# A Sin activation with its quarter turn as a number, and a skip term seeded into the bank by TensorE

## The chip, the cores and the metric

The kernel runs on one core of a Trainium2 chip. The metric is the device time of one launch in microseconds. The kernel before takes 934.82 us (median of three runs, 934.5 to 937.22).

## The reference

One block of a network on 2048 positions of 640 channels, all in fp32: an adaptive layer norm, a state-space convolution with a skip term, then a second adaptive norm and a gated feed-forward part.

```python
mod = (_silu(c) @ w_mod).reshape(c.shape[0], 6, 1, -1)          # sa, ca, ga, sb, cb, gb
h = _layernorm(x) * (1 + ca) + sa
x = x + ga * conv(h)
h = _layernorm(x) * (1 + cb) + sb
x = x + gb * ((_silu(h @ w1) * (h @ w3)) @ w2)

def conv(u):                                                     # u: [1, L, D]
    dt = exp(log_dt)[:, None]
    P = exp((dt * A)[:, :, None] * arange(L))                    # A, B, C complex, [D, 128]
    K = einsum("dn,dnl,dn->dl", C, P, dt * B).real               # one filter of length L per channel
    return causal_convolution(u, K) + u * Dskip                  # by FFT in the reference
```

Adding `Dskip` of a channel to the first tap of its filter, `K[d, 0]`, gives the same as the term `u * Dskip`.

## The kernel before

The engines are TensorE (PE; its weight loads are PEld), VectorE (DVE), ScalarE (ACT), GpSimd (POOL) and SyncE (SP, which issues most transfers). The program has two halves. Up to about 365 us it makes the filters and convolves; behind that it runs the feed-forward part in fp32r matmuls. The change touches the first half alone.

The filters are made in 40 steps (`NS`) of 16 channels (`SD`), and each step is cut into parts with two-letter names:

- `PH`: POOL multiplies the angles as integers (tile `ph`, 16 x 64 per partition). `AB`: ACT takes the absolute value into `cs`. `CO`: ACT turns `cs` into cosines in place, as Sin of a quarter turn minus the angle (`cosine`, L581). `SI`: ACT makes the sines in `ph`.
- `PA`, `XA`, `PQ`, `XQ`: PE multiplies out the exponents (banks `pa`, `pq`, which share the bank tagged B), and ACT takes Exp of them into the table `A`.
- `E1`, `E2`, `A1`, `A2`: DVE multiplies table and angles, into `E` (real parts) and `A` (imaginary parts).
- `kg` (`kgen`, L607): PE sums over the 128 states, in 32 fp32 matmuls with 32 weight columns and 64 moving columns, into one bank `pk` of [128, 4, 64]. Partition `dq * 32 + a`, group `g`, column `b` holds tap `64 a + b` (in the order of the tables) of channel `4 g + dq`.
- `K` (`k1evac`, L618): DVE adds the skip term to column 0 of each group, then multiplies the bank by the gate into the tile `K1`. `dz` is zero except on partitions 0, 32, 64 and 96, where it holds D.
- `pt`, `uk`: PE and ACT transform and store the filter; the `st`, `kc`, `T`, `Y`, `iv`, `zt` parts (tiles `p`, `kc`, `T`, `Y`, `pz`, `zt`) convolve the chunk of channels that was made before.

`pk` has one bank, so `kg` of a step waits until `K` of the step before has read it. Some parts have dummy matmuls ahead of them (`warm`: identity times identity, 128x128, into the bank that is about to be filled), to keep PE busy.

The order is written out by hand. `FRONT` is a list of words for the start (to about 128 us), which mixes the first steps with the setup, and `ROUND` is a list for a steady round of four steps. A word is a part's name, the step in the round and, behind a slash, the number of dummies. In `ROUND` the four sums stand as `kg+5`, `kg+6/1`, `kg+7` and `kg+8/2`: two with dummies and two without. `keep`, `act` and `acopy` fix each instruction at its place in its engine's order.

```python
def warm(t, n):
    ...
    for _ in range(n):
        Po.matmul(out[:, :P] if len(out.shape) == 2 else out, ident, ident, start=True, stop=True)
```

Of the kernel before, what the change touches and what calls it, by code (L numbers as in the profile page):

```python
# [9 lines left out]
F32 = mybir.dt.float32  # L10
F32R = mybir.dt.float32r
I32 = mybir.dt.int32
AF = mybir.ActivationFunctionType
OP = mybir.AluOpType
# [3 lines left out]
P = 128  # L18
# [15 lines left out]
TURN = 4294967296.0  # L34
# [51 lines left out]
def bc(ap, axis, n):  # L86
    v = ap.unsqueeze(axis)
    shape = list(v.shape)
    shape[axis] = n
    return v.broadcast_to(shape)  # L90
# [18 lines left out]
def tile_kernel(ctx: ExitStack, tc: tile.TileContext, a):  # L109
    nc = tc.nc  # L110
    V, S, G, PE = nc.vector, nc.scalar, nc.gpsimd, nc.tensor
# [7 lines left out]
    ident = cp.tile([P, P], F32, name="ident")  # L119
# [11 lines left out]
    def keep(ins):  # L131

        return tc.keep_in_program_order(ins) if in_order[0] else ins

    def act(*args, **kw):

        return tc.keep_in_program_order(S.activation(*args, **kw))  # L137
# [20 lines left out]
    kp = ssm.enter_context(tc.tile_pool(name="kp", bufs=1, side="right"))  # L158
# [2 lines left out]
    gaT = kp.tile([P, D // 4], F32, name="gaT")  # L161
    dz = kp.tile([P, D // 4], F32, name="dz")
    V.memset(dz, 0.0)
    hp = kp.tile([P, 1], F32, name="hp")
    V.memset(hp, math.pi / 2)
    sc = kp.tile([P, KD], F32, name="sc")
    cT = kp.tile([P, KD], F32, name="cT")
    uk = kp.tile([P, 3, NA, DC], F32, name="uk")
# [16 lines left out]
    pm_ = pre.enter_context(tc.tile_pool(name="pm_", bufs=1, side="right"))  # L185
# [7 lines left out]
    selx, stepx = selstep[:, :NA], selstep[:, NA:]  # L193
    s1r, c1, c1c, one4 = misc[:, :2 * NA], misc[:, 2 * NA:4 * NA], misc[:, P:P + 1], misc[:, P + 1:P + 2]
    toq, tog = misc[:, P + 2:2 * P + 2], misc[:, 2 * P + 2:]
    tiny = pm_.tile([P, 1], F32, name="tiny")
    V.memset(tiny, -1e-35)


    flat = [uk[:, i].rearrange("p f d -> p (f d)") for i in range(3)]  # L200
# [46 lines left out]
    def warm(t, n):  # L247

        out = t if len(t.shape) == 2 else t[:, 0] if t.shape[2] >= P else t[:, :P // t.shape[2]]
        for _ in range(n):  # L250
            Po.matmul(out[:, :P] if len(out.shape) == 2 else out, ident, ident, start=True, stop=True)

    class Polar:
# [46 lines left out]
        def turn(self):  # L300
            act(self.m, self.m, AF.Arctan)
            act(self.ag, self.g_r, AF.Sign, scale=-1.0)
            act(self.ai, self.g_i, AF.Sign, scale=-1.0, bias=tiny)

        def round1(self):
            Vo.scalar_tensor_tensor(self.aim, self.aim, 0.25 / math.pi, self.dtc, op0=OP.mult, op1=OP.mult)
# [220 lines left out]
    ph, cs, AA, EC, PK, K1 = {}, {}, {}, {}, {}, {}  # L527
# [51 lines left out]
        cs[s] = c  # L579

    def cosine(s):  # L581
        act(cs[s], cs[s], AF.Sin, scale=-2 * math.pi / TURN, bias=hp)

    def sine(s):
        sn = ph[s].bitcast(F32)
# [21 lines left out]
    def kgen(s, n=0):  # L607
        E, A = EC.pop(s), AA.pop(s)
        pk = psS.tile([P, SD // 4, NB], F32, name="pk", tag="pk", bufs=1)
        warm(pk, n)  # L610
        for g in range(SD // 4):
            for st, x in enumerate((E, A)):
                for dq in range(4):
                    keep(PE.matmul(pk[dq * 32:dq * 32 + 32, g, :], x[:, g * 4 + dq, 1, :], x[:, g * 4 + dq, 0:3:2, :],  # L614
                                   start=(st == 0), stop=(st == 1), tile_position=(0, dq * 32)))
        PK[s] = pk

    def k1evac(s):  # L618
        dst = tp.tile([P, SD // 4, NB], F32, name="K1", bufs=3)
        pk = PK.pop(s)  # L620
        keep(V.tensor_tensor(pk[:, :, 0], pk[:, :, 0], dz[:, s * 4:s * 4 + 4], op=OP.add))
        keep(V.tensor_tensor(dst, pk, bc(gaT[:, s * 4:s * 4 + 4], 2, NB), op=OP.mult))
        K1[s] = dst

# [193 lines left out]
    def conv_part(fn):  # L818
        return lambda k, *n: fn((k - LAG) // 8, (k - LAG) % 8, *n)

    parts = {"PH": phases, "AB": absph, "CO": cosine, "SI": sine, "PA": lambda k, n=0: exp_fast((k,), "B", n), "XA": fast,
             "PQ": lambda k, n=0: exp_slow((k,), "B", n), "XQ": slow, "E1": real1, "E2": real2, "A1": imag1, "A2": imag2,
             "kg": kgen, "K": k1evac, "pt": k_stage1, "uk": k_out}
    conv = {"st": conv_part(stage2), "kc": conv_part(k_copy), "T": conv_part(products), "Y": conv_part(sums),
            "iv": conv_part(inverse1), "zt": conv_part(z_store)}
# [93 lines left out]
    for word in FRONT:  # L919
# [3 lines left out]
        name, k = main.split("+") if "+" in main else (main, None)  # L923
# [48 lines left out]
    for rnd in range(NS // EB + 3):  # L972
        for word in ROUND:
            word, _, idle = word.partition("/")
            name, k = word[:2].rstrip("+-"), EB * rnd + int(word[len(word[:2].rstrip("+-")):])
# [60 lines left out]
    V, S, G, PE = (InOrder(tc, e, (in_order,)) for e in (V, S, G, PE))  # L1036
# [503 lines left out]
    for pair in range(2):  # L1540
# [24 lines left out]
        for n, f in enumerate(simple):  # L1565
            hA[f] = h_tile()
            ws = ws or plain_weights(f, ends if pair == 0 and n == 1 else None)
            end = plain("A", f, hA[f], ws, pair == 0, *((lambda: turn(4, 0, 2), lambda: turn(3, 1)) if n == 3 else ()))
            if n < len(simple) - 1:
                ws = None  # L1570
            todo = side.pop(0) if side else None
            if todo:
                with tc.issue_after(end.ins):
                    todo()
            if pair == 0 and n == 1:
                with tc.issue_after(power[0].ins):
                    for j, (x, z, st) in enumerate(early):
                        G.dma_start(xs[j], x)
# [103 lines left out]
```

## Time and profile before

| | us |
|---|---|
| median of the runs | 934.82 |
| span of the profiled execution (the page states no time beside it) | 932.9 |
| stretch from 201.3 to 227.9, one round of four steps | 26.6 |
| busy in that round: ACT, PE, DVE, POOL | 26.18, 25.28, 24.64, 14.87 |
| cosine, 40 ACTIVATEs on [128, 1024] | 45.3 busy, 1.153 each |
| addition of `dz` into `pk`, 40 on DVE | 6.4 busy, 0.159 each |
| the 2560 matmul rows of `pk` (two rows for each fp32 matmul) | 78.8 busy |

A row of the timeline gives the start, the duration, the engine, the line, the operation and the tiles, with the idle time before it and what ended that in brackets. Matmuls overlap in the pipeline, so what one costs is read from the start of one row to the start of the next, not from its duration. A row of the chain gives a start, a length and what the end of the program hung on there.

### The profile page before, as it was taken

The page shows a single profiled execution, that of the slowest core. Times are in us where ns is not written, and L with a number is a line of the kernel's source. Part 1 is how long each engine was busy: PE and PEld are TensorE (multiplying, and loading weights), DVE is VectorE, ACT ScalarE, POOL GpSimd, SP SyncE. Part 2 cuts the span into 40 slices and gives each one's busy share as a digit, 9 for nine tenths or more (in the row PEclk, how much of TensorE's full clock was granted, in tenths as well). Part 3 has the DMA queues.
Part 4 walks back from the last instruction along what each step waited for, and adds up shares of the span by engine and source line. Part 5 has one row for each costly group of instructions (what it writes and reads, how often), then busy time and mean ns, then how long its engine had stood idle before and what let it go on. Part 6 is the DMA issues. An engine that isn't in the chain of part 4 may idle for free.

```text
span 932.9 us, 21160 instructions
## 1 busy us (share of the span) xinstructions
PE 894.6 (96%) x8482; PEld 699.1 (75%) x8482; DVE 692.8 (74%) x1251; ACT 552.7 (59%) x810; POOL 282.3 (30%) x282
## 2 busy tenths in 40 slices
PE   5999889999999999999999999999999999999998
PEld 3776667767777766678888887778888888888886
DVE  6699889999999967676666656686876766664665
ACT  4899899999999843464433323466643333333432
POOL 3633465555556312134222200111632222200000
PEclk9999999999999999999999999999999999999999
DMA  8755888665655987853113117984322211203453
GB/s 253 243 198 201 264 230 223 171 162 153 177 155 149 230 223 245 211 212 99 56 49 97 55 45 201 271 258 158 86 70 85 84 57 57 57 29 99 141 169 114
DMA packets 103703, 140.79 MB, mean 151 GB/s; under 512 B 20612, under 2 KB 62788, under 8 KB 103604
## 3 DMA queue, kind: packets, MB, share of 16 engines
q1 hardware_dynamic: 99772, 129.32, 47.8%
q0 software_dynamic: 2368, 7.77, 2.6%
q10 hardware_dynamic: 1464, 2.34, 0.8%
q8 instruction: 67, 1.10, 0.5%
q14 instruction: 32, 0.26, 0.1%
HBM read 107.94 MB, written 31.46 MB: 149 GB/s over the span
## 4 chain that ended last, share of the span: by engine, by line
PE 72%; ACT 14%; DVE 5%; DMA 4%; issue 3%; SPq 1%; DVEq 0%; ACTq 0%
PE ps L103 56%; PE p L672 4%; ACT cs L137 3%; PE pz L721 3%; ACT A L137 3%; ACT ph L137 2%; PE pm L103 2%; ACT L137 2%; PE pk L614 1%; PE pq L552 1%; PE pa L541 1%; ACT kc L140 1%; DVE uk L103 1%; SPq L103 1%; ACT uk L140 1%
## 5 line engine op out<-in xcount | busy, mean ns | idle before, releaser
L103 DVE TENSOR_TENSOR s<-ps,s 128x512 f32<-128x512 f32 x138 | 94.9, 687 | 80.2 <-PE ps L103 79.7
L566 POOL TENSOR_TENSOR ph<-thi,iota 128x1024 int32<-128x1024 int32 x40 | 98.0, 2451 | 129.5 <-DVE A L604 77.5
L103 DVE TENSOR_TENSOR gl<-rw,gh 128x640 fp32r<-128x640 f32 x87 | 78.0, 897 | 64.2 <-ACT gh L103 64.2
L103 ACT CAST gh<-rw 128x640 fp32r<-128x640 f32 x87 | 63.3, 727 | 101.8 <-PE ps L103 61.5
L103 POOL TENSOR_TENSOR S<-rw 128x256 f32<-128x256 f32 x46 | 36.6, 798 | 170.7 <-DVE S0l L103 151.5
L103 PE MATMUL ps<-xA,gh 128*128 128x512 f32 x280 | 87.9, 392 | 0.1
L103 PE MATMUL ps<-gh,uh 128*128 128x512 f32 x224 | 87.5, 391 | 0.0
L103 PE MATMUL ps<-gl,uh 128*128 128x512 f32 x224 | 87.2, 389 | 0.0
L103 PE MATMUL ps<-gh,ul 128*128 128x512 f32 x208 | 81.1, 390 | 0.0
L672 PE MATMUL p<-uk,s 128*64 128x256 f32 x640 | 77.1, 383 | 0.9 <-issue 0.9
L103 PEld LDWEIGHTS ps<-xA,gh 128*128 128x128 f32 x280 | 52.1, 188 | 12.8 <-ACT xA L103 0.8
L672 PEld LDWEIGHTS p<-uk,s 128*64 128x64 f32 x640 | 43.4, 137 | 22.5 <-issue 3.4
L103 PE MATMUL ps<-xA,gl 128*128 128x512 f32 x140 | 54.5, 390 | 0.0
L103 ACT ACTIVATE s<-ps 128x512 f32<-128x512 f32 (+1 forms) x33 | 19.7, 598 | 50.5 <-PE ps L103 50.5
L600 DVE TENSOR_TENSOR A<-A,ph 128x1024 f32<-128x1024 f32 x40 | 49.0, 1226 | 0.0
L721 PE MATMUL pz<-Y,i 64*128 64x128 f32 x640 | 45.5, 281 | 3.6 <-ACT zt L140 2.0
L721 PEld LDWEIGHTS pz<-Y,i 64*128 64x128 f32 x640 | 39.3, 187 | 12.8 <-issue 7.3
L593 DVE TENSOR_TENSOR E<-A,cs 128x1024 f32<-128x1024 f32 x40 | 48.6, 1216 | 0.4
L103 PEld LDWEIGHTS ps<-gl,uh 128*128 128x128 f32 x224 | 42.1, 188 | 9.0
L103 PEld LDWEIGHTS ps<-gh,uh 128*128 128x128 f32 x224 | 42.1, 188 | 8.7
L137 ACT ACTIVATE cs<-cs,hp 128x1024 f32<-128x1024 f32 x40 | 45.3, 1153 | 0.2
L570 POOL TENSOR_TENSOR ph<-ph,phi 128x512 int32<-128x512 int32 x40 | 44.5, 1115 | 2.6
(244 smaller groups left out, 2301.6 us busy)
## 6 DMA issues: line engine op xcount, KB each, us to landing
rw<-in_w_dram SPq DMA_DIRECT2D x52, 320.0 KB, 3.0
us<-u SPq DMA_DIRECT2D x16, 640.0 KB, 4.5
s<-in_s_dram SPq DMA_DIRECT2D x40, 256.0 KB, 3.4
i<-in_i_dram SPq DMA_DIRECT2D x40, 256.0 KB, 4.0
rw<-in_wg_dram SPq DMA_DIRECT2D x31, 320.0 KB, 3.0
rw<-in_wu_dram SPq DMA_DIRECT2D x28, 320.0 KB, 3.5
uk<-us SPq DMA_DIRECT2D x32, 256.0 KB, 8.1
zs<-zt SPq DMA_DIRECT2D x32, 256.0 KB, 4.1
```

Of the source, the lines that this page charges most:

```text
L103: ins = fn(*args, **kw)
L137: return tc.keep_in_program_order(S.activation(*args, **kw))
L140: return tc.keep_in_program_order(S.copy(out, in_))
L541: keep(PE.matmul(pA[s][:, rr, :], la[r, t, :], r2[r, js, :].rearrange("p j b -> p (j b)"), start=True, stop=True, tile_position=(r.start, 0)))
L552: keep(PE.matmul(pQ[s][:, rr, :256], w[r, t, :], bc(sel[r, js], 2, NA) if i else r1[r, js, :], start=(i == 0), stop=(i == 1), tile_positio ...
L566: keep(G.tensor_tensor(p, bc(thi[:, s * SD:s * SD + SD], 2, NPH), bc(iota, 1, SD), op=OP.mult))
L570: keep(G.tensor_tensor(p[:, :, :NA], p[:, :, :NA], bc(phi[:, s * SD:s * SD + SD], 2, NA), op=OP.add))
L593: keep(V.tensor_tensor(EC[s][:, :, 1:3, :], AA[s][:, :, 1:3, :], mid(cs[s]), op=OP.mult))
L600: keep(V.tensor_tensor(A[:, :, 1:3, :], A[:, :, 1:3, :], mid(ph[s]), op=OP.mult))
L614: keep(PE.matmul(pk[dq * 32:dq * 32 + 32, g, :], x[:, g * 4 + dq, 1, :], x[:, g * 4 + dq, 0:3:2, :], start=(st == 0), stop=(st == 1), tile ...
L672: keep(PE.matmul(p2[par * 64:par * 64 + 64, pi, c, :], s2[:, pi * 2 + par, c * 64:c * 64 + 64], uk[:, 0:kn + 1:kn, f, :], start=True, stop ...
L721: ins = keep(PE.matmul(pz[:, par, (g % 2) * 2 + pi, :], i1[r, pi, c, :], Y[r, pi, c, :], start=(c == 0), stop=(c == 1), tile_position=(par ...
```

## The change

Three edits. The cosine's quarter turn becomes a number in the instruction, and so does the tiny bias of a Sign; the tiles `hp` and `tiny` that held them, and their memsets, go. DVE's addition of `dz` goes. In its place a matmul of the identity (weights) and four columns of `dz` writes the skip term into column 0 of each group of `pk`, with the flag that starts a sum over the whole bank; the 32 matmuls behind it add to the bank and none of them starts a sum.

```diff
-    hp = kp.tile([P, 1], F32, name="hp")
-    V.memset(hp, math.pi / 2)
...
-    tiny = pm_.tile([P, 1], F32, name="tiny")
-    V.memset(tiny, -1e-35)
...
-            act(self.ai, self.g_i, AF.Sign, scale=-1.0, bias=tiny)
+            act(self.ai, self.g_i, AF.Sign, scale=-1.0, bias=-1e-35)
...
-        act(cs[s], cs[s], AF.Sin, scale=-2 * math.pi / TURN, bias=hp)
+        act(cs[s], cs[s], AF.Sin, scale=-2 * math.pi / TURN, bias=math.pi / 2)
...
         warm(pk, n)
+        keep(PE.matmul(pk[:, :, 0], ident, dz[:, s * 4:s * 4 + 4], start=True, stop=True))
         for g in range(SD // 4):
             for st, x in enumerate((E, A)):
                 for dq in range(4):
                     keep(PE.matmul(pk[dq * 32:dq * 32 + 32, g, :], x[:, g * 4 + dq, 1, :], x[:, g * 4 + dq, 0:3:2, :],
-                                   start=(st == 0), stop=(st == 1), tile_position=(0, dq * 32)))
+                                   start=False, stop=(st == 1), tile_position=(0, dq * 32),
+                                   skip_group_check=True))
...
         pk = PK.pop(s)
-        keep(V.tensor_tensor(pk[:, :, 0], pk[:, :, 0], dz[:, s * 4:s * 4 + 4], op=OP.add))
         keep(V.tensor_tensor(dst, pk, bc(gaT[:, s * 4:s * 4 + 4], 2, NB), op=OP.mult))
```

No other instruction changes its place. On PE, at a sum without dummies in a steady round, there stood, behind ACT's release of the bank for `pa`:

```order
L541 MATMUL pa<-r_96,la 128x512 [waits Activation_49]
L541 MATMUL pa<-r_96,la 128x512
L614 MATMUL pk<-E 32x64 [waits DVE_49]
L614 MATMUL pk<-E 32x64 x3
L614 MATMUL pk<-A 32x64 x4
```

and now stands:

```order
L537 MATMUL pa<-r_94,la 128x512 [waits Activation_49]
L537 MATMUL pa<-r_94,la 128x512
L607 MATMUL pk<-dz,ident 128x4 [waits DVE_49]
L611 MATMUL pk<-E 32x64 x4
L611 MATMUL pk<-A 32x64 x4
```

The wait for DVE has gone over to the new matmul, and the sum follows it without a wait of its own. On DVE, at the evacuation of one step, there stood:

```order
L593 TENSOR_TENSOR E<-A,cs 128x16x64 [waits PE_49,Activation_49]
L621 TENSOR_TENSOR pk<-pk,dz 128x4 [waits PE_49]
L622 TENSOR_TENSOR K_3510<-pk,gaT 128x256 [waits DVE_49]
L689 TENSOR_TENSOR T<-p_3463,kc 128x512 [waits PE_49,Activation_49]
L690 TENSOR_TENSOR p_3463<-p_3463,kc 128x4x128 [waits DVE_49]
```

and now, at the same step:

```order
L589 TENSOR_TENSOR E<-A,cs 128x16x64 [waits PE_49,Activation_49]
L619 TENSOR_TENSOR K_3507<-pk,gaT 128x256 [waits PE_49]
L686 TENSOR_TENSOR T<-p_3460,kc 128x512 [waits PE_49,Activation_49]
L687 TENSOR_TENSOR p_3460<-p_3460,kc 128x4x128 [waits DVE_49]
L693 TENSOR_TENSOR Y<-T,p_3460 128x2x128 [waits DVE_49]
```

The multiplication by the gate now waits for PE itself.

## The prediction

> **What bounds the kernel now.** I read the page first, then the busy times by stretch, then the chain of work that ended last, and after that the timeline of one round, engine by engine.
>
> ```profile
> span 932.9 us, 21160 instructions
> ```
>
> All that is edited lies in the first 335 us. So the sum is made by stretches there, and what comes later is taken to move as one piece. The page gives a span of 932.9 us and no time of its own for the profiled execution; the median of the runs is 934.82 us, 1.9 us longer, and I add the sum to that median.
>
> ```profile
> 64.00:100.00 36.00, 34.09 (x622) 24.97 (x626) 35.52 (x72) 35.77 (x47) 13.42 (x13) 1.00 0.50 185
> 201.30:227.90 26.60, 25.28 (x489) 19.11 (x490) 24.64 (x40) 26.18 (x32) 14.87 (x9) 1.00 0.58 157
> 307.80:335.00 27.20, 25.71 (x502) 19.95 (x502) 23.38 (x41) 16.98 (x21) 4.19 (x7) 1.00 0.91 224
> ```
>
> The columns are the stretch, its length, and then the busy time of PE, PEld, DVE, ACT and POOL. From 64 to 100 us DVE and ACT are both full. In a steady round (four steps in 26.6 us) ACT is busy 26.18 and PE 25.28: two engines compete to be the bound, and the chain must say how.
>
> ```profile
> 59.20 2.10 ACT cs L137 x2
> ...
> 118.32 3.14 ACT cs L137 x3
> ...
> 131.59 1.03 PE pk L614 x64
> ...
> 139.74 0.42 PE pk L103 x2
> 140.16 1.03 PE pk L614 x64
> ...
> 159.84 0.59 issue
> ...
> 167.14 1.03 PE pk L614 x64
> ...
> 174.69 1.28 ACT L137
> ...
> 217.35 1.16 PE pz L721 x16
> ...
> 219.97 0.42 PE pk L103 x2
> 220.39 1.03 PE pk L614 x64
> ...
> 224.91 0.44 PE pq L552 x4
> 225.38 0.60 ACT A L137
> ...
> 307.81 1.28 ACT L137
> ```
>
> From 129.6 to 172 us the chain lies almost wholly on PE and holds six of the blocks named `pk`, from the one at 131.59 to the one at 167.14. From the table load at 174.69 to the one at 307.81 there are five equal rounds of 133.12 / 5 = 26.62 us. In each the chain is on ACT for the sines and cosines, then on PE from `pz` (217.35) to the end of `pq` (224.91 + 0.44) with one `pk` block, then on ACT again.
>
> **The change part by part.**
>
> *The cosine.* Forty ACTIVATEs lose the column `hp` as an operand.
>
> ```profile
> L137 ACT ACTIVATE cs<-cs,hp 128x1024 f32<-128x1024 f32 x40 | 45.3, 1153 | 0.2
> L137 ACT ACTIVATE cs<-ph 128x1024 f32<-128x1024 int32 x40 | 42.1, 1053 | 1.1 <-POOL ph L570 0.8 <-DVE E L596 0.3
> 208.88 1.15 ACT L137 ACTIVATE cs<-cs,hp 128x1024 f32<-128x1024 f32 x1
> 209.93 1.06 ACT L137 ACTIVATE cs<-ph 128x1024 f32<-128x1024 int32 x1
> 210.87 0.58 ACT L140 COPY kc<-p 128x512 f32<-128x512 f32 x1
> ```
>
> The absolute value, of the same size and without a column, takes 1053 ns against 1153. From start to start it is 1.05 us after the cosine (208.88 to 209.93) and 0.94 after the absolute value, so a cosine gives back about 0.10 us (the trace has no cosine with a number for its bias; at worst it gives nothing) of ACT's time, 0.38 in a round of four, all of it in the stretch where the chain is on ACT. The two Sign instructions with `tiny` gain as little each, and the two MEMSETs stand at the start, where DVE has its first loads to wait for: I cost both at nothing, and 0.2 us if that is wrong.
>
> *DVE's addition of D.* Forty small additions go.
>
> ```profile
> 87.52 0.16 DVE L621 TENSOR_TENSOR pk<-pk,dz 128x4 f32<-128x4 f32 x1
> 87.71 0.42 DVE L622 TENSOR_TENSOR K<-pk,gaT 128x256 f32<-128x256 f32 x1
> 82.00:106.50 24.50, 0.47 (x3) 1.00 0.55 188
> ```
>
> Each holds DVE for 0.19 us (87.52 to 87.71). In the steady rounds DVE has 2 us to spare, so 0.76 us a round buys nothing there. Where DVE is full it counts: three of them stand between 82 and 106.5 us.
>
> *TensorE's seed.* One matmul is added ahead of each `pk` block: 128x128 identity as weights, four columns of `dz`. The profile has no such row; the nearest are the matmuls with one column and the dummies (each fp32 matmul shows as two rows).
>
> ```profile
> 27.12 0.61 PE L103 MATMUL pm<-misc,part 128*128 128x1 f32 x4
> 27.58 0.47 PE L103 MATMUL pa<-ident 128*128 128x128 f32 x2
> ...
> 114.20 0.83 PE L103 MATMUL pm<-misc,part 128*128 128x1 f32 x6
> 114.95 0.39 PE L552 MATMUL pq<-r,la 64*128 64x256 f32 x2
> ...
> 206.41 0.71 PE L103 MATMUL pk<-ident 128*128 128x128 f32 x4
> 207.06 0.32 PE L614 MATMUL pk<-E 128*32 128x64 f32 x8
> ```
>
> Two one-column matmuls take 0.46 us when a matmul of the same tile follows (27.12 to 27.58), 0.23 each. Three take 0.75 when another tile shape follows (114.20 to 114.95), so the last costs 0.75 - 0.46 = 0.29. A block without dummies ahead of it pays that: I take 0.30. One dummy of 128 columns takes 0.42 with the change of shape behind it (219.97 to 220.39), two take 0.65 (206.41 to 207.06). So a further wide matmul costs 0.23, and ending on a narrow one saves 0.42 - 0.29 = 0.13: behind a dummy the seed costs about 0.11. The bounds are 0.11 to 0.42 for a lone seed and 0.02 to 0.23 behind a dummy, and I take the values of the narrow rows because four columns are nearest to one. A round has two of each kind: 2 x 0.30 + 2 x 0.11 = 0.82 us. The wait for DVE's reading of the bank of the step before moves from the block to the seed, one matmul earlier, so nothing new is waited for, and DVE now frees the bank 0.19 us sooner: no cost.
>
> The Trainium skill's page "TensorEngine Tiling (Array Packing)", under Key Properties, says that a change of tiling mode drains TensorE. By that rule a lone seed pays one drain more than before, which is what speaks against this change; it gives no price, the step from 0.23 to 0.29 and 0.42 above is how this trace shows it, and the sum stays as it is.
>
> *What PE has to spare.* In a round:
>
> ```profile
> 216.45 0.50 PE L541 MATMUL pa<-r,la 64*128 64x512 f32 x2 [0.23 <-ACT A L137]
> 217.35 1.16 PE L721 MATMUL pz<-Y,i 64*128 64x128 f32 x16 [0.40 <-ACT zt L140]
> 218.28 0.39 PE L552 MATMUL pq<-r,la 64*128 64x256 f32 x2
> 219.47 0.50 PE L541 MATMUL pa<-r,la 64*128 64x512 f32 x2 [0.69 <-ACT A L137]
> 217.19 1.04 ACT L137 ACTIVATE A<-pa 128x1024 f32<-128x1024 f32 x1
> ```
>
> ```profile
> PE pa L541 <- ACT A L137: 0.9, 2, 0.7
> PE pz L721 <- ACT zt L140: 0.4, 1, 0.4
> ```
>
> The second list holds all that PE waited for between 202.6 and 229.2 us (in total, times, longest).
>
> PE waits 1.32 us in all, and from 219.47 round to 0.23 us before the next round's 216.45 it waits for no other engine. Not all of the 1.32 can be used. `pa` and `pq` share one bank: ACT must read `pq` before the next `pa` starts, which keeps the 0.69. Between `pa` at 216.45 and `pq` at 218.28 stands ACT's 1.04 us of reading `pa`. It begins at 217.19 though `pa` is done by 216.95, so about 0.20 can be won there, and 0.23 ahead of 216.45: 0.43 us of room for 0.82 of new work. PE becomes the bound of the whole round, and a round grows by 0.39 us. ACT's 0.38 then only makes ACT wait for PE.
>
> *The sum.*
> - Up to 129.6 us: DVE's three additions on the chain give 0.57. Of the cosines some six stand where the chain is on ACT (from 59.20 and from 118.32 on), 0.6 more. PE's blocks there take some 0.3 back. Together -0.9.
> - 129.6 to 174.7: six `pk` blocks on a chain that is on PE, three behind dummies and three alone: 3 x 0.30 + 3 x 0.11 = +1.2.
> - Five rounds: 5 x 0.39 = +1.95.
> - 307.8 to 335: five blocks, three alone and two behind dummies, 1.12 at full price; PE has 1.5 us idle there, part of it for DVE's sums, which follow PE's own work; I take +0.8.
> - Afterwards nothing is edited and the stage is handed on late: 0.
>
> That is +3.05 us: 934.82 + 3.1 = 937.9 us, a span of about 936.0. With the bounds of the seed (0.60 to 1.16 a round, so 0.17 to 0.73 of growth) the rounds give 0.9 to 3.7, the stretch before 0.9 to 1.7, the one behind 0.4 to 1.2, the front -1.3 to -0.5: 935.7 to 940.9.
>
> **The rivals.**
>
> *PE takes the seeds in its gaps and ACT stays the bound: faster.* For it speaks that ACT is the busier engine of the round (26.18 of 26.60) and that PEld is busy only 19.11 us. The rounds would give 5 x 0.38 = 1.9, the front 1.2, the rest some 0.3: 931.4 us. Against it: the seeds would have to cost under 0.05 us a round, and no row is so cheap. The Trainium skill's page "Perfetto Trace Analysis", under Identifying the Most-Contended Engine, tells to judge TensorE's room by the busy share of weight loads and not by matmuls; 19.11 of 26.60 is 72%, and by that rule this rival holds. Against it stands the same timeline: no wait on PE for 23 of the 26.6 us. Chance 0.12.
>
> *The change of shape costs nothing: no change.* If a seed costs 0.11 everywhere, as when its weights are loaded under the matmul before, a round has 0.44 of new work for 0.43 of room and stays; the six blocks cost 0.66, the end 0.3, the front gives 1.1: 934.7 us. It decides at 0.11 a seed; 0.29 at 114.20 speaks against it. Chance 0.18.
>
> *The seed is as dear as a full dummy: clearly slower.* Its four results go to every 64th word of the bank, and no matmul of this trace writes so. At 0.42 alone and 0.23 behind a dummy a round has 1.30, growth 0.87, five rounds 4.35; the stretch before 1.95, behind 1.3, the front -0.5: 941.9 us. The skill's page "PSUM — Partial Sum Buffer", under Specifications (TRN2), warns that a pattern that is not contiguous slows matmuls significantly; no run here shows it. Chance 0.10.
>
> **How the numbers follow.** The forecast has 0.60. Less than 0.3% either way (2.8 us, 932.0 to 937.6) is about what a measurement of this kernel can't tell from no change. The forecast's middle lies just beyond it, so I give 0.36 of the 0.60 to slower and 0.24 to no change. Slower is then 0.36 + 0.10 = 0.46; no change 0.24 + 0.18 + 0.02 from the fast rival's weak side = 0.44; faster 0.10. The range leaves out the fast rival's number and the dear one's: 933.0 to 941.0.
>
> **What the profile after would show.** Cosines of about 1.05 us. No DVE addition into `pk`. Per step one seed of two rows, with the `pk` block starting 0.3 us behind it. Rounds of about 27.0 us between table loads, the chain on PE nearly throughout, PE's waits for `zt` gone, and ACT waiting for PE some 0.8 us a round. At 129.6 us the work should be about 0.9 early, at 307.8 about 2.2 late. Rounds of 26.2 us would show the first rival, 26.6 the second, 27.5 the third. A stall of another kind, such as the 0.6 us without a cause inside a `pk` block at 159.84, could add or take a microsecond and prove nothing.

## The result, and the profile after

The changed kernel takes 939.12 us (median of 10 runs, 936.94 to 942.51) against 935.09 us of the kernel before in the same measurement (10 runs, 932.98 to 937.22): a ratio of 1.0045, 95% interval 1.0031 to 1.0059. It is slower by 0.45%, a little more than can be told from no change.

The page of the changed kernel, and its busy times by stretch (the columns as in the prediction), give for the profiled execution:

```profile
span 936.3 us, 21268 instructions
```

```profile
202.50:229.86 27.36, 26.14 (x512) 20.46 (x500) 25.83 (x36) 26.14 (x33) 14.76 (x9) 1.00 0.60 156
311.91:341.79 29.88, 29.09 (x560) 23.08 (x550) 24.53 (x40) 17.86 (x23) 4.54 (x8) 1.00 0.75 206
```

The first row is one round, from table load to table load: 27.36 us where it was 26.62. PE is busy 0.86 us longer (26.14 against 25.28), and so, against what anyone would expect who takes work away from DVE, is DVE: 25.83 against 24.64.

ScalarE's timeline has the table loads that end and begin the five rounds:

```profile
175.15 1.28 ACT L137 ACT_TABLE_LOAD   x1
...
311.91 1.28 ACT L137 ACT_TABLE_LOAD   x1
```

(311.91 - 175.15) / 5 = 27.35 us a round. Round lengths below are worked out in the same way, from the same two table loads of each trace. By stretches:

| stretch (from table load to table load) | before, us | after, us | change | predicted |
|---|---|---|---|---|
| up to the load at 126.3 | 126.30 | 126.26 | -0.04 | -0.9 |
| to 174.7 | 48.39 | 48.89 | +0.50 | +1.2 |
| five rounds | 133.12 | 136.76 | +3.64 | +1.95 |
| to the load at 337.9 | 30.13 | 29.88 | -0.25 | +0.8 |
| the rest | 594.91 | 594.48 | -0.43 | 0 |
| span | 932.9 | 936.3 | +3.4 | +3.05 |

(The last row goes by spans of 932.86 and 936.27. The stretches of the prediction ended at 129.6 and 335, up to 3.3 us away from these loads.) The sum came out nearly; its parts did not. Outside the rounds each figure is from one trace of each kernel, and two kernels whose order is the same up to there (the two without tile-shaped seeds that copy ahead of the wrong product, below) reach the load of 126 at 126.58 and 126.89: a difference of 0.3 us there is scatter. The chain of work that ended last shows a round:

```profile
206.96 1.02 PE pt L630 x16
207.98 0.64 PE pk L103 x4
208.62 0.12 PE pk L607 x2
208.74 1.07 PE pk L611 x64
209.82 0.26 issue
210.07 1.95 PE p L669 x16
212.02 1.09 PE pq L103 x8
213.11 0.42 PE pq L548 x4
213.53 0.89 PE pz L718 x16
214.43 0.32 PE pk L607 x2
...
222.18 0.12 PE pk L607 x2
...
228.70 0.31 PE pk L607 x2
```

It lies on PE nearly throughout, as expected. The four seeds (L607) cost 0.12 behind dummies and 0.32 and 0.31 alone, 0.87 us together. What was not expected is the 0.26 of "issue" ahead of `p`. The list of what PE waited for in this round has it as well:

```profile
PE pa L537 <- ACT A L137: 0.7, 1, 0.7
PE p L669 <- PE pk L611: 0.3, 1, 0.3
PE pq L548 <- ACT A L137: 0.2, 1, 0.2
```

The wait for `zt` is gone, and a wait of `p` is new. The list names PE's own sums as its end, but these were done at 209.8. `p` is written into the one bank that DVE's sums `Y` of the step before still read, and in DVE's timeline these end at 209.56 + 0.41 = 209.97, just ahead of 210.07:

```profile
203.51 1.22 DVE L596 TENSOR_TENSOR A<-A,ph 128x1024 f32<-128x1024 f32 x1
204.89 2.96 DVE L589 TENSOR_TENSOR E<-A,cs 128x1024 f32<-128x1024 f32 x1 [0.16 <-ACT cs L137]
207.78 0.68 DVE L686 TENSOR_TENSOR T<-p,kc 128x512 f32<-128x512 f32 x1
...
209.56 0.41 DVE L694 TENSOR_TENSOR Y<-T,p 128x256 f32<-128x256 f32 x1
```

```profile
204.87 1.90 POOL L562 TENSOR_TENSOR ph<-thi,iota 128x1024 int32<-128x1024 int32 x1 [1.92 <-ACT cs L137]
```

One product `E` a round takes 2.96 us. In the kernel before it took 1.23, and POOL's product was the long one:

```profile
202.53 1.22 DVE L600 TENSOR_TENSOR A<-A,ph 128x1024 f32<-128x1024 f32 x1
203.79 1.23 DVE L593 TENSOR_TENSOR E<-A,cs 128x1024 f32<-128x1024 f32 x1
```

```profile
203.89 2.89 POOL L566 TENSOR_TENSOR ph<-thi,iota 128x1024 int32<-128x1024 int32 x1 [1.99 <-ACT cs L137]
```

Whoever starts first runs at its own pace, and the other ends nearly its own full length after that: before, `E` began 0.10 us ahead of POOL, and POOL ended 1.76 us after `E` did (its product takes 1.90 when it comes first). After, POOL began 0.02 us ahead, and `E` ended 1.08 us after POOL did (`E` takes 1.23 when it comes first). So small a lead proves little by itself; the test of it is the run that holds POOL back (below). Why the order turned: POOL's product starts 0.14 us after the end of DVE's `A` in both kernels, since `A` is the last to read the buffer it writes; `E` follows `A` but needs the cosine too. Before, the 0.19 us of the addition of D stood ahead of `A`, so that `A` and the cosine ended together (203.75 and 202.61 + 1.15 = 203.76). Without it `A` ends at 204.73, 0.13 us before the cosine (203.80 + 1.06 = 204.86), and POOL is let in. The two cosines, before and after:

```profile
202.61 1.15 ACT L137 ACTIVATE cs<-cs,hp 128x1024 f32<-128x1024 f32 x1
```

```profile
203.80 1.06 ACT L137 ACTIVATE cs<-cs 128x1024 f32<-128x1024 f32 x1
```

The groups of the page count it: the sum of all 40 such `E`, after, and before:

```profile
L589 DVE TENSOR_TENSOR E<-A,cs 128x1024 f32<-128x1024 f32 x40 | 59.1, 1479 | 1.1 <-ACT cs L137 1.1
L137 ACT ACTIVATE cs<-cs 128x1024 f32<-128x1024 f32 x40 | 41.6, 1057 | 0.2
```

```profile
L593 DVE TENSOR_TENSOR E<-A,cs 128x1024 f32<-128x1024 f32 x40 | 48.6, 1216 | 0.4
```

Six of the 40 are the long ones: one in each of the five rounds and one at 150.19, ahead of them. The theory to be tested: a round grew by 0.73 us because the seeds need 0.87, PE had 0.43 of room, and 0.30 of new waiting for DVE comes on top, from the place that the removed addition had held. The rival: the 0.73 are PE's own work, and the long `E` is beside the path.

### The profile page after: what moved, and what is told of

It reads as the page before. It is cut to its first block, busy times and chain, and to the rows that moved or that the text cites. A ratio compares the mean times of both kernels' runs of the same rounds, so it can differ in the third digit from the quotient of the medians.

```text
span 936.3 us, 21268 instructions
## 1 busy us (share of the span) xinstructions
PE 902.4 (96%) x8562; PEld 711.1 (76%) x8562; DVE 699.0 (75%) x1209; ACT 550.5 (59%) x810; POOL 277.7 (30%) x282
## 4 chain that ended last, share of the span: by engine, by line
PE 83%; ACT 6%; DVE 4%; DMA 2%; issue 2%; POOL 1%; SPq 0%; ACTq 0%; DVEq 0%; POOLq 0%
PE ps L103 54%; PE p L669 8%; PE pk L611 4%; PE pt L630 3%; PE pz L718 3%; PE pa L537 2%; ACT A L137 2%; PE pm L103 2%; PE pq L548 2%; PE pu L103 1%; PE pq L103 1%; PE pa L103 1%; PE pk L103 1%; ACT cs L137 1%; DMA us<-u 1%
## 5 line engine op out<-in xcount | busy, mean ns | idle before, releaser
L562 POOL TENSOR_TENSOR ph<-thi,iota 128x1024 int32<-128x1024 int32 x40 | 92.3, 2309 | 135.5 <-DVE A L600 88.1
L589 DVE TENSOR_TENSOR E<-A,cs 128x1024 f32<-128x1024 f32 x40 | 59.1, 1479 | 1.1 <-ACT cs L137 1.1
L566 POOL TENSOR_TENSOR ph<-ph,phi 128x512 int32<-128x512 int32 x40 | 49.7, 1243 | 2.6
L137 ACT ACTIVATE A<-pa 128x1024 f32<-128x1024 f32 x40 | 40.9, 1023 | 7.9 <-PE pa L537 6.9
```

The source lines that it names most:

```text
L562: keep(G.tensor_tensor(p, bc(thi[:, s * SD:s * SD + SD], 2, NPH), bc(iota, 1, SD), op=OP.mult))
L566: keep(G.tensor_tensor(p[:, :, :NA], p[:, :, :NA], bc(phi[:, s * SD:s * SD + SD], 2, NA), op=OP.add))
L589: keep(V.tensor_tensor(EC[s][:, :, 1:3, :], AA[s][:, :, 1:3, :], mid(cs[s]), op=OP.mult))
```

## The experiments

Twelve kernels, compared with the kernel before on the same chip, 12 runs each (7 of the seed alone). "Long E" counts the products `E` of 2.87 us or more (the last two kernels each have one of 1.97 and 1.82 behind the rounds besides).

| kernel | round, us | long E | ratio to before, 95% interval |
|---|---|---|---|
| before | 26.62 | 0 | 1 |
| after | 27.35 | 6 | 1.0045 (1.0031 to 1.0059) |
| numbers alone | 26.27 | 0 | 0.9971 (0.9955 to 0.9987) |
| seed alone | 27.36 | 6 | 1.0065 (1.0036 to 1.0093) |
| no skip term | 26.92 | 6 | 1.0002 (0.9986 to 1.0019) |
| after, DVE padded | 26.99 | 0 | 1.0036 (1.0019 to 1.0054) |
| copy ahead of the wrong product | 27.36 | 6 | 1.0040 (1.0016 to 1.0064) |
| copy ahead of the wrong product, tile-shaped seeds | 27.04 | 6 | 1.0035 (1.0011 to 1.0058) |
| copy ahead of the wrong product, no dummies in the rounds | 27.22 | 6 | 1.0034 (1.0011 to 1.0056) |
| copy ahead of the wrong product, both | 26.96 | 6 | 1.0012 (0.9986 to 1.0038) |
| after, POOL behind E | 26.99 | 0 | 1.0026 (1.0012 to 1.0041) |
| POOL behind E, no dummies in the rounds | 26.41 | 0 | 0.9991 (0.9978 to 1.0004) |
| POOL behind E, no dummies, tile-shaped seeds | 26.24 | 0 | 1.0013 (0.9985 to 1.0041) |
| no skip term, POOL behind E | 26.26 | 0 | 0.9985 (0.9966 to 1.0004) |

The round lengths tell most: kernels that ought to agree do so to 0.01 us, while the runs of one kernel scatter by some microseconds.

**Numbers alone.** The first of the three edits, on the kernel before:

```diff
-        act(cs[s], cs[s], AF.Sin, scale=-2 * math.pi / TURN, bias=hp)
+        act(cs[s], cs[s], AF.Sin, scale=-2 * math.pi / TURN, bias=math.pi / 2)
```

> The kernel before with the numbers for the biases alone; DVE still adds D, no seed. My theory (before, ACT is the bound of a round, PE has about 0.43 us of room in it): four cosines give 0.38 us of ACT, so the five rounds go from 26.62 to about 26.25 us (-1.9 us), the front gives about 0.6 more, the E products of DVE stay at 1.22 us; in all 2.0 to 3.0 us under the kernel before. Rival (PE is already the bound, or the stages are handed on at the same time anyway): rounds stay at 26.6, within 0.7 us of the kernel before.

Rounds of 26.27, 0.36 shorter, and 932.68 us against 935.05: as the theory said. The same stretch in its trace:

```profile
200.97:227.24 26.27, 25.24 (x489) 19.16 (x490) 24.63 (x40) 25.85 (x32) 14.79 (x9) 1.00 0.59 158
```

ACT is down by 0.33 (26.18 to 25.85) and the round by as much: ACT was the bound before. This version has the lowest ratio of all, 0.3% under the kernel before. Its interval overlaps that of the best kernel with a seed (0.9991), so it is not shown to be faster than that one.

**Seed alone.** The kernel after with the columns back:

```diff
-        act(cs[s], cs[s], AF.Sin, scale=-2 * math.pi / TURN, bias=math.pi / 2)
+        act(cs[s], cs[s], AF.Sin, scale=-2 * math.pi / TURN, bias=hp)
```

> The kernel after with the columns for the biases put back: the seed alone. My theory (PE is the bound after the change): ACT's 0.38 us a round more only uses up its waiting for PE, so the rounds stay at 27.3 to 27.4 us, and only the front loses about 0.6: 0 to 1.2 us above the kernel after. DVE reaches its E product still earlier against the cosine, so POOL starts first and one E a round takes about 2.96 us. Rival (the cosines still count in full): rounds of 27.7, 2.5 us above the kernel after.

Rounds of 27.36, the same as after to 0.01 us, though ACT has its column to read again (26.40 busy of 27.35). So ACT is not the bound of the changed kernel, and the first edit buys nothing in its rounds. The long `E` is there. The 0.6 us expected in the front did not show: the load of 126 stands at 126.39 against 126.26, a difference within the scatter.

**No skip term.** The kernel after with neither seed nor addition:

```diff
-        keep(PE.matmul(pk[:, :, 0], ident, dz[:, s * 4:s * 4 + 4], start=True, stop=True))
...
-                                   start=False, stop=(st == 1), tile_position=(0, dq * 32),
-                                   skip_group_check=True))
+                                   start=(st == 0), stop=(st == 1), tile_position=(0, dq * 32)))
```

> Leaves out the skip term: no seed and no addition of D, numbers for the biases. Theory one (one E a round takes 2.96 us because DVE, without its 0.19 us addition, ends A before the cosine is ready, and POOL starts in between): the long E is there without any seed, and PE, which has 0.8 us less to do than in the kernel after, takes some of the delay up: rounds of 26.2 to 26.6 us, 3.5 to 6 us under the kernel after. Theory two (the seed on PE shifts the engines so that E meets POOL): E takes 1.22 us, rounds of 26.2.

Theory one was right on the long `E` and wrong on the round: the six long `E` are there without a seed, and PE does not take the delay up (its wait for `p` is 0.7). The round is 26.92, not 26.2 to 26.6: 0.65 above the numbers alone, from which it differs only by DVE having less to do. The time, 934.51 us, is 4.6 under after (measured on another occasion). Its DVE row beside that of POOL:

```profile
202.70 2.97 DVE L589 TENSOR_TENSOR E<-A,cs 128x1024 f32<-128x1024 f32 x1 [0.16 <-ACT cs L137]
```

```profile
202.69 1.90 POOL L562 TENSOR_TENSOR ph<-thi,iota 128x1024 int32<-128x1024 int32 x1 [1.62 <-ACT cs L137]
```

POOL leads by 0.01 us in the record, and `E` waits.

**After, DVE padded.** The 0.19 us come back without the work:

```diff
         pk = PK.pop(s)
+        keep(V.tensor_tensor(pad, pk[:, :, 0], dz[:, s * 4:s * 4 + 4], op=OP.add))
         keep(V.tensor_tensor(dst, pk, bc(gaT[:, s * 4:s * 4 + 4], 2, NB), op=OP.mult))
```

> The kernel after, with one more DVE addition of the same size ahead of each K that reads four columns of the bank and writes them to a small column nobody reads: DVE's 0.19 us come back and the seed stays. Theory (the round grew by 0.73 us, 0.87 of seeds less 0.43 of room and 0.30 of PE's new wait for DVE behind the long E): E is back at 1.22 us, PE's wait for p is gone, rounds of 27.0 to 27.1 us, 1.2 to 1.8 us under the kernel after. Rival (the growth is PE's own work; PE had only 0.14 us of room): rounds stay at 27.35 and the time within 0.5 us of the kernel after, whatever E does.

```profile
202.82:229.81 26.99, 26.07 (x512) 20.24 (x500) 24.39 (x40) 26.02 (x32) 14.94 (x9) 1.00 0.62 158
```

Forty useless additions make the round 0.36 us shorter. `E` is back at 1.23, PE's waits are the two of 0.7 and 0.2, and the median is 1.7 us under that of after (937.45; measured on other occasions). PE's busy time is nearly that of after (26.07 against 26.14); what went is the wait. The rival falls.

**POOL behind E, a miss and then the test.** The padding changes DVE's times, so the other way was to leave DVE as it is in the kernel after and hold POOL back, by a copy of one element of `E`, which POOL can make only when `E` is done. The first try had the wrong step:

```diff
     def phase_turns(s):
         p = ph[s] = tp.tile([P, SD, NPH], I32, name="ph", bufs=4)
+        if s % 4 == 1 and s - 3 in EC:
+            keep(G.tensor_copy(pad[:, 0:1], EC[s - 3][:, 0, 1, 0:1]))
```

> The kernel after, with a copy of one column of E on POOL ahead of the first phase product of each round, so that POOL starts behind that E instead of beside it; DVE's work is that of the kernel after. Theory (E takes 2.96 us because POOL began 0.02 us ahead of it; what DVE lost is only the occasion): E takes 1.22 us, PE's wait for p is gone, rounds of 27.0 us as with the padded DVE, 1.5 to 2 us under the kernel after. Rival (POOL then meets DVE's products from p instead and they grow by as much): rounds of 27.2 to 27.4.

That product is another of the four of a round; the long `E` stayed and the round with it, 27.36. It tells only that such a copy on POOL costs nothing. Two kernels of the same batch rest on it and still have the long `E`:

> As the one with POOL behind E, and the seed done by four matmuls in the tile shape of the sums (32 columns of the identity each) instead of one of 128x128. Theory (a lone seed's 0.31 us is 0.12 of its own and 0.19 for the change of tile shape): seeds of 0.11 to 0.12 us everywhere, PE's round shorter by 2 x 0.19, rounds of 26.6 us, 1.5 to 2 us under the one with POOL behind E alone. Rival (the price is the writing of every 64th word, or a matmul's fixed cost, which is now paid four times): lone seeds of 0.3 us or more, rounds of 27.0 or more.

> As the one with POOL behind E, without the three dummies a round that stand ahead of seeds (one ahead of the second, two ahead of the fourth block). Theory (PE is the bound, so what it is spared shows in full until ACT binds at about 26.25): PE is spared 3 x 0.23 = 0.69 us, rounds of 26.3 us, about 3.5 us under the one with POOL behind E alone. Rival (the dummies keep TensorE's clock up, or the blocks wait for DVE there anyway): a granted clock under 0.99 or rounds above 26.7.

The tile-shaped seed is

```diff
-        keep(PE.matmul(pk[:, :, 0], ident, dz[:, s * 4:s * 4 + 4], start=True, stop=True))
+        for dq in range(4):
+            keep(PE.matmul(pk[dq * 32:dq * 32 + 32, :, 0], ident[:, dq * 32:dq * 32 + 32], dz[:, s * 4:s * 4 + 4],
+                           start=True, stop=True, tile_position=(0, dq * 32)))
```

and its price stands in PE's timeline, at a sum without dummies:

```profile
218.63 0.24 PE L611 MATMUL pk<-dz,ident 128*32 128x4 f32 x8
218.71 0.30 PE L616 MATMUL pk<-E 128*32 128x64 f32 x8
```

Four matmuls in 0.08 us from start to start, where the one of 128x128 took 0.31 to 0.32. They write the same every 64th word, so that is not what the lone seed paid for. Whether it paid for leaving the tile shape and coming back, or for its two weight loads of full width, no run tells apart: those two are recorded with 0.30 us (at 214.36 in the trace of after), the eight narrow ones with 0.16 (at 218.63 here). Both rounds missed what was expected. The tile-shaped seeds shortened the round by 0.32 only, and taking out three dummies, 0.69 us of PE, by 0.14: what PE was spared came back as its wait for `p`, 0.6 and 0.7 us instead of 0.3. With the long `E` in the chain a shorter PE does not help. Both together:

> All three: POOL behind E, seeds in the tile shape of the sums, no dummies ahead of seeds in the rounds. Theory: PE's own round falls to about 25.6 us, so ACT binds again at 26.2 to 26.3 us, no more than 0.1 us a round under the one without dummies; total within 1 us of the numbers alone (0.997 of the kernel before), a little less if DVE's three additions in the front pay. Rival (PE still binds): rounds of 25.6 to 25.9.

A miss: 26.96, and no more than 26.92 was to be had, which is the round with no seed at all.

The right place for the copy is behind the `E` that grew:

```diff
     def real1(s):
...
+        if s % 4 == 1:
+            keep(G.tensor_copy(pad[:, 0:1], EC[s][:, 0, 1, 0:1]))
```

> The kernel after, with POOL's copy of one column of E put right behind the E that grew (in the kernel with POOL behind E before it stood ahead of the phase product of another step, and E kept its 2.97 us). Theory as there: E takes 1.22 us, POOL's product starts after it, PE's wait for p is gone, rounds of 27.0 us as with the padded DVE. Rival (POOL's later product meets T and the sums instead): rounds of 27.2 to 27.4.

```profile
206.36 1.23 DVE L590 TENSOR_TENSOR E<-A,cs 128x1024 f32<-128x1024 f32 x1 [0.16 <-ACT cs L137]
```

```profile
207.65 0.18 POOL L592 COPY pad<-E 128x1 f32<-128x1 f32 x1 [3.23 <-DVE E L590]
207.79 1.91 POOL L563 TENSOR_TENSOR ph<-thi,iota 128x1024 int32<-128x1024 int32 x1
```

`E` starts 0.16 us after `A`, as late as in the kernel after, and takes 1.23. The round is 26.99, the same as with the padded DVE. So it is the meeting with POOL and nothing else about the addition. The total gains less than the rounds, and the front shows a reason: the traces with this copy reach the load of 126 at 128.46 and, without dummies, 128.89, the five with the same seed and no copy behind `E` between 126.26 and 126.91. The copy in the rounds alone was not tried.

**No dummies, and tile-shaped seeds, on top.** In the order of words of a round:

```diff
-kg+6/1 ... kg+8/2
+kg+6 ... kg+8
```

> The same without the three dummies a round ahead of seeds. With the long E these bought only 0.14 us a round (27.22), since PE then waited the longer for DVE. Theory: with E at 1.22 us PE is the bound until ACT binds, so the 0.69 us show: rounds of 26.3 to 26.4 us. Rival (the blocks behind the dummies waited for DVE anyway): 26.8 or more.

> The same with seeds in the tile shape of the sums. PE's round falls by a further 0.4 to 0.8 us, under ACT's: rounds of 26.0 to 26.25 us, that is the kernel with the numbers alone less what DVE's addition still costs on its chain (0.0 to 0.2). Total 0.996 to 0.999 of the kernel before.

The same edit that bought 0.14 with the long `E` buys 0.58 without it (26.99 to 26.41). PE was the bound of the 26.99, and a seed can stand in for a dummy: the granted clock of that round is 1.00 without the three. With tile-shaped seeds too the round is 26.24, 0.02 under the numbers alone, and its chain lies mostly on ACT. The total of the last kernel missed what was expected, 1.0013 against 0.996 to 0.999, by what happens outside the rounds (last section).

**No skip term, POOL behind E.** The copy behind `E`, in the kernel without skip term:

```diff
-        keep(PE.matmul(pk[:, :, 0], ident, dz[:, s * 4:s * 4 + 4], start=True, stop=True))
...
+        if s % 4 == 1:
+            keep(G.tensor_copy(pad[:, 0:1], EC[s][:, 0, 1, 0:1]))
```

> Leaves out the skip term, as the one before (numbers, no seed, no addition of D), and has POOL's copy of a column of E behind the E that grew. Theory (of the 0.65 us a round by which that kernel was above the numbers alone, all is the long E): E at 1.22 us, ACT is the bound, rounds of 26.1 to 26.27 us, about 0.996 of the kernel before. Rival (without DVE's addition something else is late too): rounds of 26.5 or more.

26.26: all of the 0.65 was the long `E`. The total is 0.9985, not 0.996; here too the front is longer with the copy (the load of 126 at 127.02 against 124.62).

## Why the prediction was right, and where it was not

- *The cosine.* 0.10 us each was predicted, 1153 to 1057 ns is measured; the rounds of the numbers alone are shorter by 0.36 of the 0.38.
- *The seed's price.* 0.82 us a round predicted, 0.87 measured: 0.12 behind dummies (0.11), 0.31 to 0.32 alone (0.30). Four columns written to every 64th word cost no more than one column did. The Trainium skill's "TensorEngine Tiling (Array Packing)", Key Properties, says that a change of tiling mode drains TensorE; 0.08 us for the seed in the tile shape of the sums against 0.31 outside it fits that, and does not show that a drain is what costs the difference. The range in the prediction took 0.60 to 1.16 us a round, where its own bounds for the two kinds of seed give 0.26 to 1.30; the 0.87 lies in both.
- *PE's room and the new bound.* 0.43 of room and a growth of 0.39 predicted. Without the long `E` the round grows by 0.37 (26.62 to 26.99, twice), PE's waits go from 1.32 to 0.92, and ACT's 0.36 vanish in ACT's waiting for PE. This step was right. The round of 27.35 itself lay nearer to the 27.5 that the prediction gave as the sign of a dear seed than to its 27.0, and the work was 4.1 us late at the end of the five rounds, not 2.2: both for the reason that follows.
- *DVE's addition* is the step that failed. "In the steady rounds DVE has 2 us to spare, so 0.76 us a round buys nothing there": it does not buy nothing, it costs 0.36 us a round with the seed and 0.65 without, because the addition had kept DVE's product `E` 0.10 us ahead of POOL's. The term for five rounds, 1.95, measured 3.64, and 1.8 of that is this. Both starts could be read in the trace of before (203.79 and 203.89), and POOL's 2.89 for a product of which one a round took 2.29 was a sign that the two disturb each other. The Trainium skill's "SBUF — State Buffer", Who interferes with whom, has the mechanism: a VectorE instruction with two inputs in SBUF and a GpSimd instruction that reads SBUF exclude each other, and who starts first blocks the other until it is done. The four rows above agree: the second ends 1.76 or 1.08 us after the first, nearly the 1.90 or 1.23 that it takes undisturbed.
- *The front, the stretch after it and the end* were predicted as -0.9, +1.2 and +0.8 and measured as -0.04, +0.50 and -0.25. Three stalls of PE without any wait lie in them. Weight loads of before, then of after:

```profile
160.43 0.15 PEld L614 LDWEIGHTS pk<-A 128*32 128x32 f32 x5 [0.75 <-issue]
...
320.86 0.15 PEld L614 LDWEIGHTS pk<-E 128*32 128x32 f32 x7 [1.23 <-issue]
```

```profile
107.62 0.15 PEld L103 LDWEIGHTS pm<-uk,scb 128*32 128x32 f32 x7 [0.75 <-issue]
```

  Before loses 0.75 in the second stretch and 1.23 in the fourth, and after loses neither; after loses 0.75 in the front, where its work had been 0.84 ahead (table load at 108.53 against 109.37). Taking the three out gives -0.8, +1.25 and +1.0. So the terms may be right, which is not shown: no run took a stall away alone, and a stall's length varies (at 160.44 in the numbers alone it is 1.16). DVE's three additions on the chain of the front, 0.57 in the prediction, can be read from two kernels: without skip term the load of 126 comes at 124.62, with the numbers alone at 125.26, 0.64 apart, of which 0.3 may be scatter.
- So 937.9 for a measured 939.1 is in part luck: by the table, 1.7 us too little in the rounds and 1.3 too much elsewhere.
- *The rivals.* ACT as the bound falls by the seed alone (ACT's 0.38 back, no change of the round) and by the dummies (PE spared 0.69, 0.58 gained). By the busy share of weight loads, which the Trainium skill's "Perfetto Trace Analysis", Identifying the Most-Contended Engine, names for this beside a measure of useful work (MFU), TensorE would be unbound at 75% (20.46 of 27.36), so here the measurement decides against that share. The change of shape that costs nothing falls by the lone seed's 0.31 against 0.12 behind a dummy, the seed as dear as a full dummy by the same two against 0.42 and 0.23.

## What to carry to other kernels

Before taking work from an engine that has time to spare, look at who starts next to its following instruction: a lead of 0.1 us can decide which of two engines waits, and the loser may be the one on the path. Judge an engine by its waits inside the stretch and not by its busy share, then count new work against those waits. In these rounds a small extra matmul was cheapest in the tile shape of its neighbours, and could take the place of a dummy; in the total the tile shape won nothing here.

## What the runs showed that was not expected

- DVE's `E` and POOL's product exclude each other nearly in full: POOL's ends 1.76 us after `E` when `E` leads, `E` 1.08 us after POOL's when POOL leads. A recorded lead of 0.01 us went with the second order.
- PE's stalls without a wait seem to belong to places in its instruction stream. The seven kernels with the 128x128 seed stall at the same instruction of that `pm` block between 107.5 and 110.3 us (by 0.47 to 1.17 us), before and the numbers alone at 160.43 and 160.44 in the same `pk` block. The DMA engines are busy nearly all the time around the first of them (a share of 0.99 or more from 100 to 112 us in the trace of after), but in the trace of before, with 0.93 or more there, that stall is missing. What the stalls are stays open.
- A stall there may cost much more than itself. In the first kernel with tile-shaped seeds it falls just ahead of a wait for DVE, and the granted clock (the third column from the right) drops behind it; the next table load stands at 122.08, where the like kernel with 128x128 seeds has it at 117.57:

```profile
104.00:108.00 4.00, 1.62 (x77) 1.29 (x80) 0.82 (x1) 3.98 (x4) 3.90 (x3) 1.00 1.07 356
108.00:112.00 4.00, 4.00 (x37) 2.94 (x29) 2.75 (x4) 1.54 (x2) 0.01 (x1) 0.55 1.10 332
```

  PE is busy 1.62 of 4 us, and then has 0.55 of its clock; in the kernel after it is busy 2.69 of those 4 us and keeps 1.00. The stall alone does not do it: the second kernel with tile-shaped seeds stalls at the same place (0.87 us, at 105.71), is busy 2.28 of those 4 us and keeps 1.00. In the last kernel, whose profiled run took 943.00 us, the clock falls to 0.63 between 108 and 112 us and to 0.51 from 112 to 130. That is the likely reason why its times scatter from 932.48 to 943.61, where those of the same kernel with 128x128 seeds lie between 931.60 and 934.08. It is not shown, since a kernel with 128x128 seeds (copy ahead of the wrong product, no dummies in the rounds) also has runs from 934.53 to 945.44.
